# The fifth head pair of a top-k attention kernel without folded rows, and working rows in other buffers

## Chip, core and metric

One NeuronCore of a Trainium2 chip. The metric is the device time of one execution in microseconds. Its engines are PE (TensorE, matmuls; its weight loads are listed as PEld), DVE (VectorE), ACT (ScalarE), POOL (GpSimd) and SP, whose queue issues the DMAs. Each works through its own instructions in the order of the program and waits on semaphores for the others.

## What is computed

```
scores = q @ k.T / 8                              # B=8, H=8, S=576, D=64
kth    = 32nd largest score of each row
attn   = softmax of the scores >= kth, else 0     # per row of 576
x      = attn @ v, the heads side by side         # (8, 576, 512)
u      = x + (x.T @ U @ V).T                      # rank 32 mix over the sequence
out    = u + relu(u @ w1) @ w2                    # 512 -> 2048 -> 512
```

All in float32. The small weights U, V and w1, w2 come as float64 and are turned into float32 in the kernel, block by block (`next_params`, lines 216 to 231): three passes on ACT (L174, L175, L178), a shift on DVE (L186), two additions on POOL (L187, L189).

## The kernel before

Two heads of one batch entry make a pair, so there are 32 pairs, `g` = 0 to 31. A pair's 576 rows are cut into five row tiles, `t` = 0 to 4: four of 128 rows for both heads (two rows of 576 scores in each partition, `n` = 2), and a last one that holds the 64 leftover rows of both heads (one row in each partition). One step of the loop at lines 770 to 883 takes one row tile: step n is tile (n // 5, n % 5). Pair 4, the fifth, has steps 20 to 24; it is the first pair of the second batch entry. `ALONE` is 20: steps 0 to 19 run the first four pairs with no MLP behind them; steps 19 and 20 have a branch of their own (780 to 817); from then on the MLP of the batch entry that is done (`mlp`, 640 to 688) is dealt out as filler on PE by `fill` (742 to 760), a share to each call, by count and not by time. Its two matmul loops are L650 (u @ w1) and L669 (@ w2). So PE has filler from step 20 on.

A row tile passes through these stages, and a step issues stages of several tiles interleaved:

- `scores(g, t)` (312 to 358): PE multiplies (L322) into PSUM tiles `sc`; ACT copies to SBUF `Ssb`: L356 to L358 for pairs 0 to 4, L349 for the pairs from 5 on, which are `blocked` (line 285: g > 4; their q and k are laid out by a DVE transpose, L292, and their columns in another order), L339 for the last tile of any pair. Called one step ahead of `front`.
- `fold(g, t)` and `split(g, t)` (365 to 390): for folded pairs, each row of 576 is turned into 288 maxima `upper` and 288 minima `lower` of two halves: POOL adds the halves as integers (L387, in `fold`), DVE takes the maximum (L389, in `split`), POOL subtracts it from the sum (L390). L389 reads its first half from PSUM where `fronts_of` has it, which is set for blocked pairs and for each pair's last tile; else it reads both from SBUF. Both are called a step ahead of `front`, in the middle of the tile before; L389 thus lies in DVE's queue among that tile's passes.
- `front(g, t)` (409 to 499): the 32nd largest value of each row, in DVE instructions that find eight maxima (MAX8) or strike eight values out (MATCH_REPLACE8). Unfolded: MAX8 over 576 (L443), then three times a strike over 576 (L455) and a MAX8 (L460); the first strike writes to working rows `places`, so that the scores stay whole, and the later ones work in them. Folded: two MAX8 and a strike over `lower` (288; L429, L431, L433) put 16 candidates behind the 288 of `upper`, and then the same passes run over 304 values. A generator: each `next` issues one part. After the last MAX8, ACT scales the threshold (L482) and makes a gap for each row (L485), POOL takes it off (L488), ACT takes the exponential (L394). The first four pairs use other ways for some rows (`ways`, 396 to 404).
- `turns(g, t)` (529 to 550): PE transposes the weights (L543, L548), ACT copies them to `PT` (L544, L549). From step 31 on DVE and two DMAs do most of it (`blocks`).
- `values(g, t)` (558 to 590): PE multiplies with v (L577, L581; L567 for the last tile); ACT copies on (L590, L575). `inverse` (552 to 556) gives the reciprocals of the sums on DVE.
- `mixed(g, wait)` (593 to 638): the rank 32 mix of a pair (L602, L613, L625, L627 on PE; L606, L621, L635 on ACT).

Pools matter here. `hT` is a ring of 10 buffers of 128 x 640 floats that holds the MLP's hidden rows (line 660, written by ACT at L662) and, in pairs 0 to 3, the working rows (line 437). `upper` is a ring of 2 buffers of 128 x 2 x 304 floats, used by folded pairs alone. `lower` has one buffer.

Of the kernel before, what the change touches and what calls it, by code (L numbers as in the profile page):

```python
# [8 lines left out]
F32 = mybir.dt.float32  # L9
# [5 lines left out]
TOPK = 32  # L15
# [11 lines left out]
def kernel(  # L27
# [30 lines left out]
    P = 128  # L58
# [6 lines left out]
    HALF = S // 2  # L65
    assert S == MAIN + TAIL and D == 64 and H % 2 == 0 and C == 512 and TOPK % 8 == 0
    NPAIR = H // 2
    NP = B * NPAIR
# [8 lines left out]
    HT = 10  # L77
# [5 lines left out]
    attn = ctx.enter_context(tc.tile_pool(name="attn", bufs=2))  # L83
    small = ctx.enter_context(tc.tile_pool(name="small", bufs=8))
    mlpp = ctx.enter_context(tc.tile_pool(name="mlpp", bufs=2))
# [10 lines left out]
    WIDE = 2 * P + TAIL  # L96
# [184 lines left out]
    def blocked(g):  # L281

        return g > NPAIR
# [78 lines left out]

    def fold(g, t):

        if NPAIR <= g < NP:
            upper = attn.tile([P, 2, HALF + TOPK // 2], F32, tag="upper", name="upper")
            lower = attn.tile([P, 2, HALF], F32, tag="lower", name="lower", bufs=1)
            folds[g, t] = upper, lower  # L370
            pair(g, t, 0)
# [6 lines left out]
    def pair(g, t, stage):  # L378
        S2 = S2s[g, t]
        n = S2.shape[1]  # L380
        upper, lower = folds[g, t]
        top, bottom = upper[:, 0:n, 0:HALF], lower[:, 0:n].bitcast(U32)
        a, b = S2[:, :, 0:HALF], S2[:, :, HALF:S]
        if t < NT and blocked(g):
            a, b = (ends_of(probs[g, t], i) for i in range(2))
        if stage == 0:
            nc.gpsimd.tensor_tensor(bottom, a.bitcast(U32), b.bitcast(U32), ALU.add)  # L387
        else:
            nc.vector.tensor_tensor(top, fronts_of.pop((g, t), a), b, ALU.max)  # L389
            nc.gpsimd.tensor_tensor(bottom, bottom, top.bitcast(U32), ALU.subtract)  # L390

    def weigh(chunk, E, nmax, total=None):

        nc.scalar.activation(E, chunk, AF.Exp, bias=nmax, scale=SCALE, accum_out=total)  # L394

    def ways(g, t):

        if (g, t) == (NPAIR - 1, NT - 1):
            return (0,), (), (1,)
        if (g, t) == (NPAIR - 1, NT):  # L400
            return (0,), (), ()
        if t == NT:
            return (), (), (0,)
        return ((), (1,), (0,)) if g < NPAIR else ((), (), (1, 0))
# [4 lines left out]
    def front(g, t):  # L409

        if t == 0:
            dens[g] = small.tile([P, 2 * NT + 1], F32, tag="den", name="den", bufs=3)
        S2, den = S2s.pop((g, t)), dens[g]
        n = S2.shape[1]
        chunks = [S2[:, c] for c in range(n)]
        sums = [den[:, 2 * t + c : 2 * t + c + 1] for c in range(n)]
        first = small.tile([P, 2, 8], F32, tag="first", name="first", bufs=3)  # L420
        nmax = small.tile([P, 2], F32, tag="nmax", name="nmax", bufs=4)
        order = (1, 0) if n == 2 else (0,)
        folded = (g, t) in folds
        if folded:
            upper, lower = folds.pop((g, t))
            curs = [upper[:, c] for c in range(n)]
            spots = [[upper[:, c, HALF + i : HALF + i + 8] for c in range(n)] for i in (0, 8)]
            for c in order:
                nc.vector.max(spots[0][c], lower[:, c])  # L429
            for c in order:  # L430
                nc.vector.match_replace(lower[:, c], spots[0][c], lower[:, c], NEG)  # L431
            for c in order:
                nc.vector.max(spots[1][c], lower[:, c])  # L433
        else:
            curs = list(chunks)
            places = [
                mlpp.tile([P, 2, WIDE], F32, tag="hT", name="hT", bufs=HT)
                .rearrange("p c n -> p (c n)")[:, 0:S]
                for _ in range(n)
            ]  # L440
        ms = [first[:, c] for c in range(n)]
        for c in order:
            nc.vector.max(ms[c], curs[c])  # L443
        yield
        early, pooled, gaps = ways(g, t)
        for i in range(1, TOPK // 8):
            if i == 1:
                nc.scalar.mul(nmax[:, 0:n], first[:, 0:n, 0], -SCALE)
                Es = {c: attn.tile([P, S], F32, tag="E", name="E") for c in early}
                for c in early:  # L450
                    weigh(chunks[c], Es[c], nmax[:, c : c + 1])
            for c in order:

                nxt = places[c] if i == 1 and not folded else curs[c]
                nc.vector.match_replace(nxt, ms[c], curs[c], NEG)  # L455
                curs[c] = nxt
            m8 = small.tile([P, 2, 8], F32, tag="m8", name="m8", bufs=4)
            ms = [m8[:, c] for c in range(n)]
            for c in order:
                nc.vector.max(ms[c], curs[c])  # L460
            yield
        for c in pooled:
            gap = attn.tile([P, S], F32, tag="E", name="E")
            nc.gpsimd.tensor_scalar(gap, chunks[c], ms[c][:, 7:8], NEG, ALU.is_lt, ALU.mult)
            nc.gpsimd.tensor_tensor(chunks[c], chunks[c], gap, ALU.add)  # L465
        for c in early:
            nc.vector.scalar_tensor_tensor(
                out=chunks[c],
                in0=chunks[c],
                scalar=ms[c][:, 7:8],  # L470
                in1=Es[c],
                op0=ALU.is_ge,
                op1=ALU.mult,
                accum_out=sums[c],
            )
        if t == NT:
            del qkTs[g]
        yield
        if gaps:
            lo, hi = min(gaps), max(gaps) + 1  # L480
            least = small.tile([P, 2], F32, tag="least", name="least", bufs=3)
            nc.scalar.mul(least[:, lo:hi], m8[:, lo:hi, 7], WIDEN)  # L482
            for c in gaps:
                gap = attn.tile([P, S], F32, tag="E", name="E")
                nc.scalar.activation(  # L485
                    gap, chunks[c], AF.Relu, bias=least[:, c : c + 1], scale=-WIDEN
                )
                nc.gpsimd.tensor_tensor(chunks[c], chunks[c], gap, ALU.subtract)  # L488
            yield
        ahead = order[0:1] if len(gaps) == 2 else ()  # L490
        for c in ahead:
            weigh(chunks[c], chunks[c], nmax[:, c : c + 1], sums[c])
            yield
        for c in order:
            if c not in early and c not in ahead:
                weigh(chunks[c], chunks[c], nmax[:, c : c + 1], sums[c])
        if t == NT and g != NPAIR - 1:
            nc.scalar.activation(den, den, AF.Identity, bias=eps)
        yield
# [270 lines left out]
    for n in range(STEPS + 2):  # L770
        g, t = divmod(n, CH)
        if n < STEPS:
            if t == 0 and g + 1 < NP:
                load(g + 1)
            if t == 1 and g + 1 < NP:
                ready = prep(g + 1)
            fronts[n] = front(g, t)
            next(fronts[n])
        here, last = fronts.get(n, iter(())), fronts.pop(n - 1, iter(()))
        if n >= ALONE - 1 and n <= ALONE:  # L780

            if n < ALONE:
                next(last)
                values(*divmod(n - 3, CH))
                list(turning)
                next(here)
                next(last)
                scores(*divmod(n + 1, CH))
                fold(*divmod(n + 1, CH))
                values(*divmod(n - 2, CH))  # L790
# [11 lines left out]
            fill()  # L802
            scores(*divmod(n + 1, CH))
            fold(*divmod(n + 1, CH))
            next(here)
            while mixing:
# [12 lines left out]
        if n < ALONE:  # L819
            if ease:  # L820
                next(last, None)
            scores(*divmod(n + 1, CH))
            fold(*divmod(n + 1, CH))
            if n >= 3:
                values(*divmod(n - 3, CH))
                if (n - 3) % CH == NT:
                    mixing.append(mixed((n - 3) // CH, 3))
            list(turning)
            fill()
            next(here)  # L830
            if t < NT - 1:
                next_params(1)
            fill()
            next(ready, None)
            next(here)
            next(last, None)
            fill()
            split(*divmod(n + 1, CH))
            next(here)
            if t in (0, 1, NT - 1):  # L840
                next_params(1)
            next(here)
            fill()
            if n >= 1:
                turning = turns(*divmod(n - 1, CH))
            continue
# [70 lines left out]
```

## Time and profile before

| | |
|---|---|
| Median of 3 runs | 1743.06 us (1742.22 to 1745.01) |
| The profiled execution | 1742.03 us; its span 1740.2 us |
| Mean granted PE clock | 0.971 of full |
| L387 and L390 (POOL, fold) | 140 instructions each, means 1296 and 1287 ns |
| L389 in pair 4, both halves in SBUF | 0.76, 1.78, 1.80, 1.56 us |
| L443 over 576 values (unfolded) | 36 instructions, median 742 ns |
| L443 over 304 values (folded) | 252 instructions (126 rows of the list), median 459 ns |

The profile's second part cuts the span into 40 slices of 43.5 us and gives each engine's busy share in tenths. The waits name an instruction, what it waited for, and how long. The timelines list the instructions of one engine by start time. Two instructions in a row overlap a little in them, so that what one costs is best read from its start to the next one's start. Steps 20 to 24 take the stretch from about 203 to 256 us.

### The profile page before, as it was taken

The page shows a single profiled execution, that of the slowest core. Times are in us where ns is not written, and L with a number is a line of the kernel's source. Part 1 is how long each engine was busy: PE and PEld are TensorE (multiplying, and loading weights), DVE is VectorE, ACT ScalarE, POOL GpSimd, SP SyncE. Part 2 cuts the span into 40 slices and gives each one's busy share as a digit, 9 for nine tenths or more (in the row PEclk, how much of TensorE's full clock was granted, in tenths as well). Part 3 has the DMA queues.
Part 4 walks back from the last instruction along what each step waited for, and adds up shares of the span by engine and source line. Part 5 has one row for each costly group of instructions (what it writes and reads, how often), then busy time and mean ns, then how long its engine had stood idle before and what let it go on. Part 6 is the DMA issues. An engine that isn't in the chain of part 4 may idle for free.

```text
span 1740.2 us, 29711 instructions
## 1 busy us (share of the span) xinstructions
PE 1634.9 (94%) x9489; PEld 1208.1 (69%) x9489; DVE 1494.1 (86%) x4358; ACT 1023.9 (59%) x2582; POOL 956.7 (55%) x759
## 2 busy tenths in 40 slices
PE   4566789999999999999999999999999999999999
PEld 2344556777677876778677776687667876687677
DVE  7999889899999999999999999999999999993000
ACT  4888788665655666565656665565656656563100
POOL 4778688656555555555555555556555555552000
PEclk7788899999999999999999999999999999999999
DMA  3332222344434444444444444444444444432010
GB/s 87 91 90 83 73 73 64 78 111 119 119 99 116 117 114 107 112 116 105 118 101 117 114 111 105 112 111 115 110 107 119 114 109 103 117 90 70 4 16 13
DMA packets 275837, 167.37 MB, mean 96 GB/s; under 512 B 173920, under 2 KB 260192, under 8 KB 275680
## 3 DMA queue, kind: packets, MB, share of 16 engines
q1 hardware_dynamic: 274624, 165.20, 36.8%
q8 instruction: 75, 1.23, 0.3%
q14 instruction: 82, 0.67, 0.1%
q10 hardware_dynamic: 1056, 0.26, 0.1%
HBM read 101.42 MB, written 63.96 MB: 95 GB/s over the span
## 4 chain that ended last, share of the span: by engine, by line
PE 78%; DVE 11%; DMA 3%; ACT 3%; POOL 1%; issue 1%; SPq 1%; POOLq 0%; DVEq 0%; ACTq 0%
PE mm L669 27%; PE mm L650 26%; PE sc L322 8%; PE O L581 6%; DVE m L460 4%; DVE hT L455 4%; DMA PT<-away 2%; PE O L567 2%; PE up L625 2%; PE tp L548 1%; DVE first L443 1%; PE O L577 1%; PE tp L543 1%; DMA away<-y 1%; PE up L627 1%
## 5 line engine op out<-in xcount | busy, mean ns | idle before, releaser
L669 PE MATMUL mm<-hT,w 128*128 128x256 f32 (+1 forms) x2048 | 545.1, 411 | 0.0
L650 PE MATMUL mm<-uT,w 128*128 128x256 f32 (+1 forms) x2048 | 539.8, 411 | 0.0
L488 POOL TENSOR_TENSOR Ssb<-Ssb,E 128x576 f32<-128x576 f32 x271 | 378.7, 1415 | 283.5 <-ACT E L485 283.2
L650 PEld LDWEIGHTS mm<-uT,w 128*128 128x128 f32 x2048 | 376.0, 192 | 100.0 <-issue 13.3
L669 PEld LDWEIGHTS mm<-hT,w 128*128 128x128 f32 x2048 | 374.4, 192 | 94.7 <-issue 11.5
L460 DVE MAX8 m<-upper 128x8 f32<-128x304 f32 x756 | 323.7, 465 | 2.9
L390 POOL TENSOR_TENSOR lower<-lower,upper 128x576 uint32<-128x576 uint32 (+1 forms) x140 | 180.2, 1287 | 110.4 <-DVE upper L389 103.3
L394 ACT ACTIVATE Ssb<-Ssb,nmax 128x576 f32<-128x576 f32 x286 | 221.6, 779 | 17.4 <-POOL Ssb L465 9.6
L455 DVE MATCH_REPLACE8 upper<-m,upper 128x304 f32<-128x304 f32 x504 | 227.5, 458 | 0.0
L662 ACT ACTIVATE hT<-mm 128x320 f32<-128x320 f32 (+1 forms) x256 | 104.8, 409 | 203.5 <-PE mm L650 201.8
L387 POOL TENSOR_TENSOR lower<-Ssb 128x576 uint32<-128x576 uint32 (+1 forms) x140 | 181.5, 1296 | 69.5 <-ACT Ssb L349 23.5
L322 PE MATMUL sc<-qkT 64*128 64x288 f32 x1334 | 209.6, 437 | 8.6 <-ACT Ssb L356 7.8
L485 ACT ACTIVATE E<-Ssb,least 128x576 f32<-128x576 f32 x271 | 197.9, 769 | 5.2
L322 PEld LDWEIGHTS sc<-qkT 64*128 64x128 f32 x1334 | 115.4, 182 | 94.5 <-issue 42.6
L349 ACT COPY Ssb<-sc 128x576 f32<-128x576 f32 x216 | 127.1, 640 | 83.4 <-PE sc L322 82.1
L515 DVE STREAM_TRANSPOSE y<-Ssb 128x512 f32<-128x512 f32 x208 | 142.9, 702 | 22.8 <-ACT Ssb L394 20.9
L581 PE MATMUL O<-PT,va 128*64 128x128 f32 x2048 | 145.0, 285 | 8.5 <-DMA PT<-away 8.5
L429 DVE MAX8 upper<-lower 128x8 f32<-128x288 f32 x252 | 103.0, 445 | 38.3 <-POOL lower L390 38.3
L581 PEld LDWEIGHTS O<-PT,va 128*64 128x64 f32 x2048 | 113.5, 141 | 25.5 <-DMA PT<-away 10.8
L682 DVE TENSOR_TENSOR oT<-uT,mm 128x320 f32<-128x320 f32 (+1 forms) x8 | 3.6, 454 | 144.1 <-PE mm L669 144.1
L590 ACT COPY XT<-O 128x128 f32<-128x128 f32 x128 | 34.2, 267 | 143.3 <-PE O L581 143.2
L455 DVE MATCH_REPLACE8 upper<-first,upper 128x304 f32<-128x304 f32 x252 | 114.0, 459 | 0.0
(95 smaller groups left out, 2068.7 us busy)
## 6 DMA issues: line engine op xcount, KB each, us to landing
away<-y SPq DMA_DIRECT2D x416, 128.0 KB, 2.4
PT<-away SPq DMA_DIRECT2D x104, 512.0 KB, 3.3
raw<-in_moe_w_ch_dram SPq DMA_DIRECT2D x32, 512.0 KB, 3.9
va<-in_v_dram SPq DMA_DIRECT2D x64, 128.0 KB, 2.3
out_dram<-ob SPq DMA_DIRECT2D x57, 128.0 KB, 2.0
ld<-in_q_dram SPq DMA_DIRECT2D x108, 64.0 KB, 2.7
ld<-in_k_dram SPq DMA_DIRECT2D x108, 64.0 KB, 2.4
ld<-in_q_dram SPq DMA_DIRECT2D x108, 8.0 KB, 2.3
```

What stands on the lines that cost most here:

```text
L322: nc.tensor.matmul(out, lhsT=qkT[half(h), 0, cols(t)], rhs=qkT[half(h), 1, lo:hi], start=True, stop=True,)
L387: nc.gpsimd.tensor_tensor(bottom, a.bitcast(U32), b.bitcast(U32), ALU.add)
L390: nc.gpsimd.tensor_tensor(bottom, bottom, top.bitcast(U32), ALU.subtract)
L394: nc.scalar.activation(E, chunk, AF.Exp, bias=nmax, scale=SCALE, accum_out=total)
L455: nc.vector.match_replace(nxt, ms[c], curs[c], NEG)
L460: nc.vector.max(ms[c], curs[c])
L485: nc.scalar.activation(gap, chunks[c], AF.Relu, bias=least[:, c : c + 1], scale=-WIDEN)
L488: nc.gpsimd.tensor_tensor(chunks[c], chunks[c], gap, ALU.subtract)
L515: nc.vector.transpose(y[:, :, h].rearrange("p r c j -> p c r j"), E2[:, a : a + MAIN].rearrange("p (c r j) -> p c r j", c=NT, r=4),)
L581: nc.tensor.matmul(O[half(h)], lhsT=va[:, h, j, :], rhs=PB[:, h, j] if shared(g, t) else PT[:, NT * h + j], start=False, stop=(j == NT - 1),)
L650: nc.tensor.matmul(ph[:, 0:w], lhsT=w1[:, cc, f * P : (f + 1) * P], rhs=uT[:, cc, lo:hi], start=(cc == 0), stop=(cc == NC - 1),)
L669: nc.tensor.matmul(po[:, 0:w], lhsT=w2[:, f, c * P : (c + 1) * P], rhs=hTs[f][:, 0:w], start=(f == 0), stop=(f == NF - 1),)
```

## The change

Two lines. Pair 4 is no longer folded: `fold` takes the blocked pairs alone, which are those from 5 on, so `split` finds nothing for pair 4, and `front` goes its unfolded way there. The working rows of all unfolded pairs, now pairs 0 to 4, are taken from the ring `upper` of the pool `attn` and no longer from the ring `hT` of `mlpp`; of each buffer's 608 columns the first 576 are used. Nothing else in the program differs; the numbers of buffers are the same.

```diff
     def fold(g, t):
 
-        if NPAIR <= g < NP:
+        if blocked(g) and g < NP:
             upper = attn.tile([P, 2, HALF + TOPK // 2], F32, tag="upper", name="upper")
             lower = attn.tile([P, 2, HALF], F32, tag="lower", name="lower", bufs=1)
             folds[g, t] = upper, lower
@@
         else:
             curs = list(chunks)
             places = [
-                mlpp.tile([P, 2, WIDE], F32, tag="hT", name="hT", bufs=HT)
+                attn.tile([P, 2, HALF + TOPK // 2], F32, tag="upper", name="upper")
                 .rearrange("p c n -> p (c n)")[:, 0:S]
                 for _ in range(n)
             ]
```

## The prediction

> **What bounds the kernel now.** I read the busy shares first, then busy time in stretches of 5 us around the fifth pair (pair 4; its five row tiles are steps 20 to 24), then the waits there, then each engine's timeline.
>
> ```profile
> PE 1634.9 (94%) x9489; PEld 1208.1 (69%) x9489; DVE 1494.1 (86%) x4358; ACT 1023.9 (59%) x2582; POOL 956.7 (55%) x759
> PE   4566789999999999999999999999999999999999
> DVE  7999889899999999999999999999999999993000
> ```
>
> PE is the bound from about slice 6 on; before that DVE is full and PE is not. The fifth pair lies in the crossing (198 to 256 us). Time saved there reaches the end only as PE idle time removed: afterwards PE runs nearly without a gap (1480.9 of 1500 us from 240 on) in a fixed order.
>
> ```profile
> 195.00:200.00 5.00, 3.21 (x31) 2.13 (x27) 1.46 (x4) 3.89 (x10) 2.90 (x3) 1.00 0.34 53
> ...
> 220.00:225.00 5.00, 5.00 (x27) 3.27 (x26) 5.00 (x14) 3.63 (x8) 3.11 (x4) 1.00 0.00 0
> 225.00:230.00 5.00, 1.45 (x8) 0.78 (x6) 5.00 (x15) 3.71 (x8) 3.05 (x3) 1.00 0.36 105
> 230.00:235.00 5.00, 3.38 (x19) 2.46 (x21) 5.00 (x16) 3.66 (x11) 5.00 (x5) 0.65 0.36 107
> 235.00:240.00 5.00, 5.00 (x19) 3.35 (x16) 4.11 (x10) 2.34 (x7) 4.17 (x3) 0.67 0.15 45
> ```
>
> (PE, PEld, DVE, ACT, POOL busy us, then PE's granted clock.) PE loses 5.2 us in 225 to 235, and right after it runs at half clock.
>
> ```profile
> DVE upper L429 <- POOL lower L390: 14.0, 6, 4.7
> ...
> ACT least L482 <- DVE m L460: 4.9, 3, 2.6
> ...
> DVE upper L389 <- ACT Ssb L358: 3.5, 1, 3.5
> ```
>
> (195 to 330 us: who waited for whom, total us, times, longest.) The timelines of DVE, ACT and PE place them; a row is start, length, engine, line, operation, and in brackets the idle time ahead of it and what ended it. (4,0) is row tile 0 of pair 4.
>
> ```profile
> 198.60 0.76 DVE L389 TENSOR_TENSOR upper<-Ssb 128x576 f32<-128x576 f32 x1 [3.54 <-ACT Ssb L358]
> ...
> 216.09 0.82 DVE L429 MAX8 upper<-lower 128x8 f32<-128x288 f32 x2 [2.27 <-POOL lower L390]
> ...
> 239.28 0.82 DVE L429 MAX8 upper<-lower 128x8 f32<-128x288 f32 x2 [0.89 <-POOL lower L390]
> ...
> 226.25 0.20 ACT L482 ACTIVATE least<-m 128x2 f32<-128x2 f32 x1 [2.62 <-DVE m L460]
> ...
> 230.24 0.33 PE L548 MATMUL tp<-ident,Ssb 128*128 128x128 f32 x1 [3.79 <-ACT PT L544]
> ...
> 233.06 0.79 PE L577 MATMUL O<-PT,vd 128*128 128x128 f32 x2 [1.39 <-ACT PT L549]
> ```
>
> DVE stands before the fold of (4,0), in the middle of tile (3,4), and before (4,1) and (4,3). Being late, it keeps ACT waiting at L482 for the last MAX8 of (4,1). Queued behind L482 on ACT is the PT copy L544 (229.58) that PE's L548 needs; so PE stands 3.79 us, and 1.39 more for L549.
>
> [...] half clock from about 200.76 to 204.17 and from 231.48 to 238.31[...]. [...] the windows just ahead had PE busy 38% and 36%; one with 53% (224.6 to 228.1) left the clock alone.
> [...] L389 with both inputs in SBUF took 1.78, 1.80 and 1.56 us under POOL work, 0.76 free of it, and a mean 0.742 where one input is in PSUM.
>
> **The change, part by part** (profiled execution; DVE from start to start).
>
> 1. *DVE work.* An unfolded two-row tile, (3,3), runs from 181.88 to 191.52: 9.64 us. A folded one, (4,1), runs from 216.09 to 226.15, less 0.32 for L186 and 1.73 for the next tile's L389: 8.01. Single rows, waits and L186 taken out: 5.64 for (3,4) (0.78 for L443, then 1.68, 1.64, 1.54 for each L455 with its L460) against 5.15 for (4,4) (0.49, 0.55, 0.50, 0.51, then 1.02, 1.04, 1.04). The five L389 take 0.68 + 1.71 + 1.73 + 1.48 + 0.35 = 5.95. Removed: 4 x 8.01 + 5.15 + 5.95 = 43.1; added: 4 x 9.64 + 5.64 = 44.2. DVE gets 1.1 us more to do. Could the wide operations stretch beside POOL? The 36 wide L443 span 731 to 761 ns beside a POOL that was 78% busy (20 to 200 us), so no: at most 0.02 each, nothing below.
> 2. *DVE waits.* 3.54 + 2.27 + 0.89 = 6.7 us go. In their place L443 waits for ACT's copy (L358). It is there at 198.57 for (4,0), which DVE reaches at 199.2: no wait. Behind it are queued the two den operations for L575.
> 3. *POOL.* Five L387 and five L390 go: 1.97+1.41+1.41+1.59+0.79 and 1.41+1.40+1.42+1.39+0.80 = 13.6 us. POOL isn't the bound, but L488 stood behind them.
> 4. *Buffers.* Working rows move from hT to the two `upper` buffers. Writers and readers are all on DVE, in order; the waits are those of before. The MLP's first Relu into hT (213.22) didn't wait for DVE before either. Nothing. No DMA, no matmul and no ACT instruction is moved; SP's queue stays.
>
> **The path, step by step.**
> Step 19: DVE goes on at 195.05 without the stop and without L389, so L467 of (3,4) ends at 199.2 instead of 203.5. But PE was busy (at half clock) with L581 and L602 until 203.68 before that tile's transposes, so they don't move. Only L575, which waited for the reciprocal until 206.94, goes at 206.6: PE shifts by 0.3.
> Step 20: DVE does (4,0) in 9.64 + 0.25 (den) + 0.32 (L186) from 199.2 to 209.4. Copy (4,1) comes at 209.7: DVE waits 0.3.
> Step 21: (4,1) to 209.7 + 9.64 + 0.4 (L186) = 219.8 instead of 226.15. ACT, full from 218.9 on, comes to L482 at 223.2 and finds it ready. Its fixed chain (L482, L485 twice 1.59; L178 0.64; three copies 1.10; L544 0.48) ends at 227.0, so L548 starts at 227.2, not 230.24. L662 0.32, the second L544 0.53, L394 0.76 and L549 follow (POOL's L488, now behind L187 and L189 alone, is done at 225.5, and no longer holds L394): L577 starts at 229.05 instead of 233.06. That is 4.0 us.
> Clock: PE's idle in this stretch is then 1.1 + 0.55 us. No 3.41 us window is under 52% busy, just where the clock was kept before. Without half clock the run from L577 to the end of L650 x12 takes 4.76 us (0.32, 1.02 and 3.42 from the later rows) instead of 7.34: 2.6 us.
> Sum: 4.0 + 2.6 = 6.6 us.
> Steps 22 to 24: is DVE late now? (4,2) ends at 219.8 + 1.28 (L292) + 0.32 + 9.64 + 0.8 (L186) = 231.8; its L482 is due at 239.76 - 6.6 = 233.1. (4,3) takes 9.64 + 0.6 + 0.32 (two L186) to 242.4; its L482 is due at 250.28 - 6.6 = 243.7. For (4,4) the margin is 2.7. Cover of 1.3 us: if DVE takes more, that comes off the gain. From step 25 on rows are folded as before and everything (ACT, POOL, DVE) hangs on PE's order, so the shift stays.
> 1742.03 (span 1740.2 and 1.8 around it) - 6.6 = 1735.4; the median of the runs is 1.03 above the profiled execution: 1736.5.
>
> **Rivals.**
> B, *the clock still drops*: 52% is between 53% (kept) and 38% (dropped), and half a microsecond of further delay on ACT decides it. Then only the wait goes: 4.0 us, 1739.1. For it: the margin is thin[...]. Against: the two idle pieces have 1.2 us of work between them.
> C, *the gain is given back*: PE still stands 2.3 us in 280 to 300 (1.54 of it at 281.8, for L544) and 4.5 in 340 to 440. [...] half clock for one or two windows costs 1.7 to 3.4, and other waits realign: some 5 us back, 1741.5. Against: those waits hang on PE's own results.
> D, *slower, DVE becomes the bound*: place, steps 20 to 24. If the removed waits for POOL come back as waits for ACT's copies, DVE has only its longer tiles: 9.64 against 8.01 + 0.68 for an L389[...], 0.95 a tile, and 0.14 for the last: 4 us later at L482 and so at PE: 1747. It decides when ACT's copies come over 6 us later against DVE than computed. Against: copy (4,2) is there at 217.3 and DVE wants it at 221.4.
> That the change does nothing is excluded: the program has 10 POOL instructions and 20 rows of DVE's listing fewer.
>
> **Chances.** Forecast 0.55, B 0.23, C 0.15, D 0.07. Forecast's own range is 1733 to 1738.5: the unknown costs are 1.3 us of cover and the clock's 2.6; the runs span 1742.2 to 1745.0, and 0.2% (3.5 us) is about what can be told from no change. The range reaches over B and part of C: 1732.5 to 1742. Faster by over 0.2% (under 1739.6): 0.55 + over half of B = 0.68; within: the rest of B and C = 0.25; slower 0.07.
>
> **What would show it.** Right: no L387 or L390 before step 24; no DVE wait of 3.5 at 195; no ACT wait at L482 near 223; L577 of (4,0) near 229; PE's clock full after 204; DVE busy in 199 to 242. Wrong: PE idle over 2 us in 225 to 230, half clock at 231, or a DVE wait for L358 of over 1 us; then (B, D) the gain shrinks. If L577 is 4 us early but the end isn't, C holds.

## The result, and the profile after

| | before | changed |
|---|---|---|
| Median, first measurement | 1744.03 us (1742.22 to 1745.91, 4 runs) | 1737.41 us (1735.06 to 1737.89, 4 runs) |
| Ratio, 95% interval | | 0.9959 [0.9942, 0.9977] |
| Median, second measurement | 1742.93 us (1741.40 to 1744.65, 9 runs) | 1736.68 us (1733.63 to 1737.09, 5 runs) |
| Ratio, 95% interval | | 0.9961 [0.9947, 0.9974] |
| Profiled execution (span) | 1742.03 us (1740.2) | 1737.48 us (1735.6) |

The changed kernel is 6 to 7 us faster: 1737.4 where 1736.5 was forecast. The two profiled executions differ by 4.6 us only. One profile is one execution: two of the changed kernel have spans of 1735.6 and 1734.3, so the sum is judged by the medians and the steps by the places in the trace.

The page of the changed kernel, first its busy time, then the shares of the slices:

```profile
PE 1631.6 (94%) x9489; PEld 1205.1 (69%) x9489; DVE 1496.6 (86%) x4317; ACT 1024.0 (59%) x2582; POOL 942.7 (54%) x749
PE   4566899999999999999999999999999999999999
DVE  7999989999999999999999999999999999993000
```

DVE works 2.5 us longer and POOL 14.0 less. In the two slices from 174 to 261 us PE goes from 7 and 8 to 8 and 9, DVE from 8 and 8 to 9 and 8. The 5 us stretches of the changed kernel (PE, PEld, DVE, ACT, POOL busy us, then PE's clock):

```profile
195.00:200.00 5.00, 3.93 (x35) 2.65 (x35) 4.83 (x13) 4.61 (x13) 1.52 (x2) 1.00 0.32 52
220.00:225.00 5.00, 4.70 (x26) 2.83 (x24) 5.00 (x10) 4.97 (x11) 2.40 (x2) 1.00 0.32 105
225.00:230.00 5.00, 3.73 (x26) 2.57 (x27) 5.00 (x12) 4.36 (x14) 4.92 (x5) 1.00 0.32 105
230.00:235.00 5.00, 5.00 (x27) 3.13 (x26) 5.00 (x11) 4.45 (x10) 2.22 (x3) 1.00 0.33 107
235.00:240.00 5.00, 5.00 (x35) 3.71 (x34) 5.00 (x12) 4.35 (x13) 3.90 (x3) 1.00 0.01 3
275.00:280.00 5.00, 2.66 (x14) 1.46 (x15) 5.00 (x16) 3.78 (x9) 4.92 (x5) 0.76 0.32 105
```

In 225 to 235 PE now stands 1.27 us where it stood 5.2, at full clock. In the last row, 40 us later, PE stands 2.3 us and the clock drops; the profile of before has a shorter stop there and full clock. In the waits of 195 to 330 the row of L389 for L358 is gone, and the ones left are of later, folded tiles but for one of 0.43 us:

```profile
DVE upper L429 <- POOL lower L390: 10.6, 4, 4.7
...
ACT least L482 <- DVE m L460: 4.0, 3, 2.3
```

The timelines of PE and ACT (start, length, line, and in brackets the idle time ahead and what ended it; the row of 283.34 is of the kernel before, the others of the changed one):

```profile
206.22 1.24 PE L322 MATMUL sc<-qkT 64*128 64x288 f32 x8
...
225.73 0.33 PE L548 MATMUL tp<-ident,Ssb 128*128 128x128 f32 x1 [1.03 <-ACT PT L544]
...
227.67 0.49 PE L577 MATMUL O<-PT,vd 128*128 128x128 f32 x2 [0.54 <-ACT PT L549]
...
232.54 1.19 PE L322 MATMUL sc<-qkT 64*64 64x288 f32 x8
...
277.20 0.71 PE L613 MATMUL pT<-x,U 128*32 128x128 f32 x10 [2.58 <-POOL w L189]
...
283.34 0.60 PE L613 MATMUL pT<-x,U 128*32 128x128 f32 x10 [1.54 <-ACT PT L544]
...
221.75 0.19 ACT L482 ACTIVATE least<-m 128x2 f32<-128x2 f32 x1
232.44 0.20 ACT L482 ACTIVATE least<-m 128x2 f32<-128x2 f32 x1 [0.43 <-DVE m L460]
```

L482 of (4,1) finds its MAX8 done, L548 waits 1.03 us instead of 3.79, and the scores of (4,4), the 64x64 row, start at 232.54 instead of 240.40. The releaser named at L613 in the changed kernel is not the true one. L613 reads x and U, which no L189 of this stretch writes, and it writes to a buffer of the ring that L544 empties. In every trace of the study this L613 starts 0.73 to 0.74 us after ACT's L544 does (here L544 at 276.47 and L613 at 277.20, before 282.60 and 283.34), while L189 only happened to end at 277.15.

What PE's lead over before is, at the same instruction in both profiles:

| instruction on PE | before | changed | lead |
|---|---|---|---|
| scores of (4,1), L322 | 207.96 | 206.22 | 1.7 |
| L577 of (4,0) | 233.06 | 227.67 | 5.4 |
| scores of (4,4), L322 | 240.40 | 232.54 | 7.9 |
| scores of (5,1), L322 | 259.44 | 252.24 | 7.2 |
| L613 of step 26 | 283.34 | 277.20 | 6.1 |
| scores of (5,4), the x10 row | 293.66 | 288.39 | 5.3 |
| span | 1740.2 | 1735.6 | 4.6 |

So between these two executions 7.9 us are won by 240, and 2.6 are given back by 290.

### The profile page after: what moved, and what is told of

It is laid out like the page before. It is cut to its first block, busy times and chain, and to the rows that moved or that the text cites. A ratio compares the mean times of both kernels' runs of the same rounds, so it can differ in the third digit from the quotient of the medians.

```text
span 1735.6 us, 29654 instructions
## 1 busy us (share of the span) xinstructions
PE 1631.6 (94%) x9489; PEld 1205.1 (69%) x9489; DVE 1496.6 (86%) x4317; ACT 1024.0 (59%) x2582; POOL 942.7 (54%) x749
## 4 chain that ended last, share of the span: by engine, by line
PE 78%; DVE 13%; DMA 4%; ACT 3%; issue 1%; POOL 1%; SPq 1%; POOLq 0%; DVEq 0%
PE mm L650 26%; PE mm L669 26%; PE sc L322 8%; PE O L581 6%; DVE upper L455 5%; DVE m L460 5%; DMA PT<-away 3%; PE O L567 2%; DVE first L443 2%; PE up L625 2%; PE tp L548 1%; PE O L577 1%; PE tp L543 1%; PE up L627 1%; DMA away<-y 1%
## 5 line engine op out<-in xcount | busy, mean ns | idle before, releaser
L488 POOL TENSOR_TENSOR Ssb<-Ssb,E 128x576 f32<-128x576 f32 x271 | 379.0, 1416 | 291.0 <-ACT E L485 290.6
L460 DVE MAX8 m<-upper 128x8 f32<-128x304 f32 (+1 forms) x864 | 407.8, 509 | 3.6
L455 DVE MATCH_REPLACE8 upper<-m,upper 128x304 f32<-128x304 f32 (+1 forms) x576 | 285.4, 502 | 0.0
L390 POOL TENSOR_TENSOR lower<-lower,upper 128x576 uint32<-128x576 uint32 (+1 forms) x135 | 173.8, 1287 | 108.8 <-DVE upper L389 101.6
L662 ACT ACTIVATE hT<-mm 128x320 f32<-128x320 f32 (+1 forms) x256 | 104.9, 410 | 201.6 <-PE mm L650 200.0
L322 PE MATMUL sc<-qkT 64*128 64x288 f32 x1334 | 209.3, 436 | 8.0 <-ACT Ssb L356 7.2
L387 POOL TENSOR_TENSOR lower<-Ssb 128x576 uint32<-128x576 uint32 (+1 forms) x135 | 174.2, 1290 | 63.1 <-ACT Ssb L349 23.2
L322 PEld LDWEIGHTS sc<-qkT 64*128 64x128 f32 x1334 | 115.1, 182 | 93.6 <-issue 42.7
L429 DVE MAX8 upper<-lower 128x8 f32<-128x288 f32 x243 | 99.2, 444 | 34.8 <-POOL lower L390 34.8
L455 DVE MATCH_REPLACE8 upper<-first,upper 128x304 f32<-128x304 f32 x243 | 109.8, 459 | 0.0
```

The source lines that it names most:

```text
L322: nc.tensor.matmul(out, lhsT=qkT[half(h), 0, cols(t)], rhs=qkT[half(h), 1, lo:hi], start=True, stop=True,)
```

## The experiments

The theories by the letters of the expectations. **W**, the prediction's: DVE's stops at folded tiles make L482 late, so PE stands at L548 and loses its clock. **P**: what counts is POOL's 14 us less. **B**: the other buffers. **H**: the longest stop, 3.5 us ahead of (4,0), is the head of the queue and worth most. **L**: what counts is L389 with both inputs in SBUF, which three times took 1.56 to 1.80 us in pair 4. **S**: DVE has slack after the change. **A**: the gap at L613 eats part of the gain. Ratios are against the kernel before, with 95% intervals; what a run saves is worked out from its ratio, and 0.001 of it is 1.7 us.

**The buffers alone.** Pair 4 folded as before, the working rows of pairs 0 to 3 in `upper`.

```diff
-                mlpp.tile([P, 2, WIDE], F32, tag="hT", name="hT", bufs=HT)
+                attn.tile([P, 2, HALF + TOPK // 2], F32, tag="upper", name="upper")
```

> Only the second half of the change: the working rows of pairs 0 to 3 lie in the two upper buffers, pair 4 is still folded. Theory W (the stops of DVE at the folded tiles delay ACT's L482, PE's gap and its half clock follow): nothing, 0 +- 1.5 us against before; the gap of 3.8 us at L548 and the half clock at 231 stay. Rival B (the buffers do it, by freeing hT for the MLP): about -6 us.

Measured: 1742.51 us, ratio 0.9996 [0.9986, 1.0005]. B falls: the second of the two edits alone does nothing that can be told. Its PE timeline:

```profile
203.59 0.63 PE L543 MATMUL tp<-ident,Ssb 128*128 128x128 f32 x4 [1.18 <-DVE Ssb L467]
...
230.78 0.48 PE L548 MATMUL tp<-ident,Ssb 128*128 128x128 f32 x1 [3.79 <-ACT PT L544]
```

The 3.79 us at L548 are those of before. The first row matters more: here PE waits 1.18 us for DVE in step 19, which the profile of before does not show. Two more places differ from the profile of before, though the kernels are equally fast:

```profile
283.11 0.60 PE L613 MATMUL pT<-x,U 128*32 128x128 f32 x10 [2.07 <-POOL w L189]
...
296.22 1.20 PE L322 MATMUL sc<-qkT 64*64 64x288 f32 x10
```

L613 waits 2.07 us and not 1.54, half clock follows from 283.9 to 290.8, and the scores of (5,4) start at 296.22 and not at 293.66. So this place changes by more than 2 us between two profiles of kernels that are equally fast.

**POOL kept busy.** The changed kernel, with additions and subtractions on POOL into an idle buffer at the places of L387 and L390.

```diff
+        elif g == NPAIR:
+            idle[g, t] = attn.tile([P, 2, HALF], F32, tag="lower", name="lower", bufs=1)
+            load_pool(g, t, 0)
...
+        elif (g, t) in idle:
+            load_pool(g, t, 1)
```

> The changed kernel, with POOL's ten instructions put back as idle work: at the old places of L387 and L390 of pair 4, POOL adds the halves and subtracts one of them again, 13 us in all, and nothing reads the result. It leaves out no part of the computation. Theory W: DVE's order is that of the changed kernel, so most of the gain stays, -4 to -6.5 us against before; up to 2 lost where POOL's weight additions and L488 come later. Rival P (the gain is POOL's relief): back to before, -1 to +1.

Measured: 1737.68 us, 0.9967 [0.9954, 0.9980]: the changed kernel's time, and the scores of (4,4) at 232.67 against 232.54. P falls.

**Only tile (4,0) unfolded.**

```diff
-        if NPAIR <= g < NP:
+        if NPAIR <= g < NP and (g, t) != (NPAIR, 0):
```

> Only row tile 0 of pair 4 unfolded, tiles 1 to 4 folded; working rows in hT as before. It takes away the longest stop of DVE (3.54 us at 195, before L389 of (4,0)). Theory W: the second stop takes its place, since L390 of (4,1) waits on POOL behind the additions L187 and L189 and is not sooner than about 215.5: (4,1) still starts near 216, L482 still waits some 2.6 us, 0 to -1.5 us against before. Rival H (the longest stop, an L389 at the head of DVE's queue in the middle of tile (3,4), is the cause): -3 to -4.5.

Measured: 1739.92 us, 0.9983 [0.9975, 0.9990], 3.0 us less. Its timelines of DVE, ACT and PE:

```profile
214.94 0.82 DVE L429 MAX8 upper<-lower 128x8 f32<-128x288 f32 x2 [2.52 <-POOL lower L390]
...
225.11 0.20 ACT L482 ACTIVATE least<-m 128x2 f32<-128x2 f32 x1 [2.64 <-DVE m L460]
...
229.10 0.47 PE L548 MATMUL tp<-ident,Ssb 128*128 128x128 f32 x1 [3.81 <-ACT PT L544]
```

The wait is W's: with the first stop gone, the second (2.52 us ahead of (4,1)) holds L482 as long as before, 2.64 us, and PE stands 3.81 us. The size is not: W had 0 to 1.5 us for this, H 3 to 4.5, and the interval is 1.7 to 4.4. In the trace the whole row of events lies 1.1 us earlier, since the scores of (4,1) start at 206.80 and not at 207.96, so the stop's own effect in step 19 was taken too small. By the scores of (4,4) the lead is 2.5 us (237.90 against 240.40), because the half clock, 227.5 to 234.3, falls in part into the gap ahead of L548.

**Only tiles (4,1) to (4,4) unfolded.** `if (blocked(g) or (g, t) == (NPAIR, 0)) and g < NP:` in `fold`, the buffers as in the change.

```diff
-        if blocked(g) and g < NP:
+        if (blocked(g) or (g, t) == (NPAIR, 0)) and g < NP:
```

> The other part: row tiles 1 to 4 of pair 4 unfolded, tile 0 folded; working rows in upper. The stop of 3.54 us at 195 stays. Theory W: (4,0) ends near 212, (4,1) follows at once and ends near 222, which is before ACT comes to L482: PE's gap at L548 falls to about 1 us, the half clock at 231 goes; then DVE is the tighter one in steps 22 and 23: -3.5 to -6 us against before. Rival H: the longest stop is still there, -1 to -3.

Measured: 1735.98 us (6 runs), 0.9959 [0.9943, 0.9975], 7.1 us less, with an interval of 4.4 to 9.9: as far as the runs can tell as much as the whole change. Its DVE, ACT and PE timelines:

```profile
198.93 0.76 DVE L389 TENSOR_TENSOR upper<-Ssb 128x576 f32<-128x576 f32 x1 [3.87 <-ACT Ssb L358]
...
223.83 0.19 ACT L482 ACTIVATE least<-m 128x2 f32<-128x2 f32 x1
...
227.82 0.33 PE L548 MATMUL tp<-ident,Ssb 128*128 128x128 f32 x1 [1.06 <-ACT PT L544]
```

H, which had 1 to 3 us for this, falls as the main cause: the longest stop is there in full, 3.87 us, and L482 waits for nothing. What has to go above all is the stop at (4,1), in the tile that L482 waits for. The stop at (4,0) still costs: the scores of (4,4) start at 234.60, against 232.54 in the changed kernel. At that place the leads over before roughly add up, 2.5 us for (4,0) alone, 5.8 for the rest alone, 7.9 for both; the medians (3.0, 7.1, and 6.2 to 7.1) are too wide to say otherwise.

**Folded, but L389 with one input from PSUM.** This kernel and the next read the first half of pair 4's rows from PSUM, where the second head's row begins with other columns. They change that part of the computation: for that head DVE's maxima are taken over other pairs of scores than POOL's sums, so what they compute for it is not what the kernel before computes. The instructions are as many, and only L389 changes its length.

```diff
+        if g == NPAIR:
+            fronts_of[g, t] = scs[0][:, :, 0:HALF]
         main = S2.rearrange("p (h n) -> p h n", h=2)
```

> The kernel before, all of pair 4 folded, but its L389 reads the first half from PSUM, as it does in later pairs, so POOL doesn't stretch it. Theory W: L389 falls from 1.7 to 0.74 us in three tiles, but the stops at 195, before (4,1) and before (4,3) stay: (4,1) ends some 1.6 us sooner, PE's gap at L548 shrinks from 3.8 to about 2: -1 to -2.5 us against before, -4 if the clock is kept. Rival L (the stretched L389 are what costs, DVE's sum of work decides): 3 us less DVE work show one to one and the gain is as large as that of the change, -5 to -7.

Measured: 1740.52 us, 0.9987 [0.9979, 0.9994], 2.3 us less. L389 shrinks to 0.73 to 0.76 us from 1.56 to 1.80. In the profile of before the three long ones (210.38, 222.76, 235.18) started beside a POOL instruction and ended 0.61 to 0.62 us after it; the one of (4,0) started 0.04 us ahead of POOL's L387 (198.60 against 198.64), so not free of POOL as the prediction has it, and took 0.76; one of pair 5, with half its input in PSUM, took 0.76 beside POOL's L488 (253.73). But the stop grows to fill much of what is won:

```profile
216.04 0.82 DVE L431 MAX8 upper<-lower 128x8 f32<-128x288 f32 x2 [3.13 <-POOL lower L392]
...
225.14 0.20 ACT L484 ACTIVATE least<-m 128x2 f32<-128x2 f32 x1 [1.03 <-DVE m L462]
```

(Lines are 2 higher here.) DVE gets to (4,1) as late as POOL's subtraction lets it; within (4,1) the shorter L389 brings L482 1.1 us forward (225.14 against 226.25). L falls as the main cause: 2.3 of 7 us, with an interval of 1.0 to 3.7.

**Tile (4,0) unfolded and the rest with L389 from PSUM.**

```diff
+        if g == NPAIR and t > 0:
+            fronts_of[g, t] = scs[0][:, :, 0:HALF]
...
+        if NPAIR <= g < NP and (g, t) != (NPAIR, 0):
```

> A mix: tile 0 of pair 4 unfolded (working rows in hT), tiles 1 to 4 folded with L389 reading from PSUM. DVE has about 3 us less to do than in the changed kernel, but the stops before (4,1) and (4,3), which wait on POOL's L390, are back. Theory W: stops count for more than work: -1 to -3.5 us against before, less than the change brings. Rival L (DVE's sum of work decides): better than the change, -7 to -9.

Measured: 1739.59 us, 0.9982 [0.9976, 0.9989], 3.1 us less. The stop ahead of (4,1) is 1.95 us long, the one ahead of (4,3) 1.34, L482 waits 0.98, and PE 2.17 at L548. Without the stretched L389 and without the first stop, about half of the gain is there (1.9 to 4.2 of 6.2 to 7.1 us), though DVE has less to do than in the changed kernel. So, by these waits, what the rest hangs on is mostly the fold's way over POOL and back.

**The clock alone.** The kernel before with matmuls that do no work of the result, in the gap ahead of L548 of (4,0). The first form wrote to a new PSUM tile:

```diff
+        if n == ALONE + 2:
+            warm = ps_m.tile([P, C], F32, tag="mm", name="mm")
+            for i in range(6):
+                nc.tensor.matmul(
+                    warm[:, 0:WIDE], lhsT=w1[:, 0, 0:P], rhs=V[:, 0:WIDE], start=(i == 0), stop=(i == 5)
+                )
```

> The kernel before with six matmuls (12 records of 0.27 us, 3.3 us in all) that nobody reads, put on PE into the gap ahead of L548 of step 22. It leaves out no part of the computation. It fills the gap with activity and takes no wait away. If half clock after the gap costs what the prediction took (2.6 us from L577 to the end of the twelve L650): half clock at 231 gone, -1.5 to -3 us against before. If the clock costs nothing, 0 to +0.5; if the six don't fit into the gap, up to +1.

Measured: 1743.73 us, 1.0006 [0.9998, 1.0013]. It tells nothing on the clock, since the gap is not filled:

```profile
231.16 5.19 PE L863 MATMUL mm<-V,w 128*128 128x320 f32 x12 [4.12 <-ACT hT L662]
```

The new tile waits for a buffer that ACT's L662 frees, and on ACT L662 stands behind L482 as well. The second form writes to columns of the tile that the MLP has open at that time, which nothing reads:

```diff
+        if n == ALONE + 2:
+            warm = opened[0][:, WIDE:C]
+            for i in range(8):
+                nc.tensor.matmul(
+                    warm, lhsT=w1[:, 0, 0:P], rhs=V[:, 0 : C - WIDE], start=False, stop=False
+                )
```

> The kernel before with eight matmuls that nobody reads (16 records of about 0.16 us, 2.6 us) in the gap ahead of L548 of step 22. Unlike the first try they write to the unused columns of the PSUM tile that is open there, so they wait for nothing on ACT. It leaves out no part of the computation, and takes no wait away. If the half clock after the gap costs what the prediction took (2.6 us from L577 to the end of the twelve L650): no half clock near 231, -1.5 to -3 us against before[...]. If the clock costs nothing: 0 +- 0.7.

Measured: 1742.27 us against 1742.03, 1.0003 [0.9995, 1.0011]. Its PE and ACT timelines:

```profile
226.84 2.76 PE L866 MATMUL mm<-V,w 128*128 128x192 f32 x16
...
283.12 0.60 PE L613 MATMUL pT<-x,U 128*32 128x128 f32 x10 [2.54 <-POOL w L189]
...
239.02 0.20 ACT L482 ACTIVATE least<-m 128x2 f32<-128x2 f32 x1 [1.04 <-DVE m L460]
```

The clock is at 1.00 from 220 to 245. From L577 (233.64) to the scores of (4,4) (238.51) it takes 4.87 us instead of 7.34, just what the changed kernel takes (227.67 to 232.54). In the runs nothing of these 2.5 us is left (0.9 us less to 1.9 more). The trace shows where they go in one execution. PE is 1.9 us ahead at the scores of (4,4), the next L482 waits 1.04 us, and 1.2 us of lead are left at 277. Then L613 stands 2.54 us, half clock follows from 284.0 to 290.8, and the scores of (5,4) start at 296.27, 2.6 us later than in the profile of before. So the kept clock alone is worth nothing at the end. That it would be worth 2.5 us if DVE were early too was not tested by itself.

**More work for DVE.** The changed kernel with one more MAX8 over 576 for each of the nine rows of pair 4, 9 x 0.66 = 5.9 us.

```diff
+        if g == NPAIR:
+            more = small.tile([P, 2, 8], F32, tag="more", name="more", bufs=2)
+            for c in order:
+                nc.vector.max(more[:, c], chunks[c])
         for c in order:
             nc.vector.max(ms[c], curs[c])
```

> The changed kernel with a MAX8 over 576 more for each row of pair 4 on DVE, nine in all, 0.66 us each (6 us), whose result nobody reads. It leaves out no part of the computation. Theory W with DVE just covered (the changed trace shows L482 waiting 0.43 us in step 22 and not elsewhere in steps 21 to 23, and POOL's L187 behind DVE's L186): the 6 us come through less about 1: +3.5 to +5.5 us against the changed kernel. Rival S (DVE has slack in these steps, PE or ACT sets the time): at most +1.5.

Measured: 1739.64 us, 0.9984 [0.9977, 0.9991]: 2.8 us less than before, so about 4 us of the gain are lost for 5.9 us of work. (L482 is L486 here.) ACT:

```profile
223.04 0.20 ACT L486 ACTIVATE least<-m 128x2 f32<-128x2 f32 x1 [0.34 <-DVE m L464]
235.99 0.20 ACT L486 ACTIVATE least<-m 128x2 f32<-128x2 f32 x1 [1.79 <-DVE m L464]
247.29 0.20 ACT L486 ACTIVATE least<-m 128x2 f32<-128x2 f32 x1 [2.09 <-DVE m L464]
```

S falls: the work comes back as waits at L482, and half clock follows from 252.3 to 259.1. The cover of steps 22 to 24 is then some 2 us, and DVE is the tight engine there after the change.

**The changed kernel once more**, for the interval and a second profile.

> The changed kernel once more, unaltered, for a narrower interval and a second profile[...]. Theory W: -5.5 to -7.5 us against before (ratio 0.9957 to 0.9969). The stop of 2.6 us before L613 near 274 is in the order of the program and is there again[...].

Measured: as in the first table. The longer gap at L613 is there again:

```profile
276.69 0.60 PE L613 MATMUL pT<-x,U 128*32 128x128 f32 x10 [2.49 <-POOL w L189]
...
279.14 1.43 PE L625 MATMUL up<-V,Tb 128*128 128x320 f32 x2 [1.01 <-ACT Tb L621]
```

Half clock follows from 279.1 to 282.5. The changed kernel with POOL kept busy waits only 1.53 us there, so this gap is not the same in all kernels with the change.

**One weight block a step later.** Ahead of the L544 that L613 waits for, ACT passes two blocks of weights in step 26 (L178 at 271.28, L174, L175, and L178 at 274.77). In the changed kernel the second is moved out of that step, in pair 5 alone:

```diff
-        if t in (1, 3):
+        if t in ((2, 3) if g == NPAIR + 1 else (1, 3)):
             next_params(1)
```

> The changed kernel, but pair 5 takes its second extra weight block in its third step instead of its second, so that step 26 has one block's three passes on ACT instead of two. The changed trace gives back 2.6 us between 274 and 288: PE stands 2.58 us before L613, for a PT copy that is queued behind those passes on ACT, and then runs at half clock. Theory A (ACT's queue in step 26 causes the give-back): the gap falls to 1 us or less, no half clock there: -2 to -3.5 us against the changed kernel, -8.5 to -10.5 against before. Rival (DVE's and POOL's chain of pair 4 and 5 sets it): 0 to -1 against the changed kernel; or, if w2 then comes too late for L669, slower by 1 to 2.

Measured: 1732.54 us (1730.62 to 1734.14, 5 runs) against 1742.03, 0.9947 [0.9933, 0.9960]: 9.2 us less. PE:

```profile
275.90 0.60 PE L613 MATMUL pT<-x,U 128*32 128x128 f32 x10 [1.56 <-ACT PT L544]
```

The gap is 1.56 us, as in the profile of before and not under 1 as expected, and the clock stays full to 300. Against the changed kernel PE is 0.3 us ahead at the scores of (4,1), 1.3 at L613 and 3.1 at the x10 scores (285.33 against 288.39): 1.0 us from the wait and 1.8 from the clock. So what is queued on ACT sets that gap, as A says, and the gap costs the changed kernel time. The size is less sure: the medians are 4 to 5 us apart, but the two weren't measured side by side, one run of the changed kernel (1733.63) lies below this kernel's slowest, and the ratios' intervals overlap. That the gap eats part of what the change won is not shown. The kernel with the other buffers alone has a gap of 2.07 us and half clock there too, and the block was not moved in the kernel before, where it may win as much.

**The same, with (4,0) folded.**

```diff
-        if blocked(g) and g < NP:
+        if (blocked(g) or (g, t) == (NPAIR, 0)) and g < NP:
...
-        if t in (1, 3):
+        if t in ((2, 3) if g == NPAIR + 1 else (1, 3)):
```

> Row tile 0 of pair 4 folded, tiles 1 to 4 unfolded, and the weight block of pair 5 moved by a step as in the run beside it. Theory A: -9 to -11 us against before, as good as or a little better than with all five unfolded. Rival: as the run without the move, about -7.

Measured: 1734.21 us (1731.91 to 1736.28, 5 runs), 0.9955 [0.9942, 0.9967]: 7.8 us less, under the 9 to 11 expected. L613 waits 1.55 us and the clock is full. The interval, 5.7 to 10.1 us, reaches into what was expected. In the trace the scores of (4,1) start 2.1 us later than in the kernel above (208.02 against 205.92) and those of (5,4) 1.8 later (287.10 against 285.33): the stop at (4,0) costs here too. The kernel above has the lowest median of the study, 1.7 us lower, but the runs of the two overlap.

## Why the prediction was right, point by point

- *DVE's work, 1.1 us more*: 2.5. The wide passes kept their length, as argued (0.66 to 0.73 us from start to start). What was off is L186: 1.04 and 1.03 us in tiles (4,0) and (4,1), where 0.3 to 0.4 was taken, 1.4 us in all. Both times POOL was at work as it started (the last section has the rows). Tile (4,1) ended at 220.73, not at 219.8. (The mean of L389 with one input in PSUM is 0.744 us and not 0.742; nothing hangs on it.)
- *DVE's stops, 6.7 us, go, and no new wait for L358*: right. DVE waits for nothing from 190 to 250.
- *POOL and buffers, nothing*: right within some 2 us, by the two runs on P and B.
- *Step 19, 0.3 us*: **the term that failed**; it was 1.7. The prediction let the transposes of (3,4) wait for PE's own work until 203.68, at half clock. That half clock (200.8 to 204.2) was of the one profiled execution. In the profiles of six other kernels that fold (4,0) the clock is full there (in four of them it is halved just after, from 205 to 209), and L543 waits 1.18 to 1.19 us for DVE's L467. So the stop does hold PE where the clock is full, and the profile of before hid it. The 0.3 us by way of L575 came (0.37); the other 1.4 are the transposes, which start at 202.31 and not at 203.68.
- *Step 21, L577 4.0 us earlier*: 5.4. Without step 19 that is 4.0 - 0.3 = 3.7 predicted and 5.4 - 1.7 = 3.7 measured.
- *The clock, 2.6 us*: 2.5 (7.34 against 4.87) between the two profiles; against the profile of the other buffers alone, where the half clock falls in part into the gap, 1.2 (6.05 against 4.87). Rival B, that it drops all the same, did not come. But as a term that adds to the others it was put too simply: by itself it is worth nothing that the runs show.
- *Steps 22 to 24, a cover of 1.3 us*: just enough. L482 of (4,2) waits 0.43 us, the others not, and PE's lead is 7.9 us at the scores of (4,4) and of (5,0) alike.
- *"From step 25 on ... the shift stays"*: **between these two profiles this failed.** Of 7.9 us, 2.6 are given back: 0.7 by 252, 1.1 at L613, and the rest behind it, where the clock is halved. PE is 7.9 us earlier, but POOL's L390 of (5,0), behind the weight blocks in its queue, only 5.9 (252.67 against 258.57), and DVE and ACT with it: L482 of (5,0) waits 2.25 us instead of 0.96. Not all hangs on PE's order. This is rival C in its place, and with its half clock, at half its price of 5 us. But the profile of before happens to keep the clock at this place. Against that of the other buffers alone, a kernel as slow as before, the lead is 7.1 us at the scores of (4,4) (239.65) and 7.8 at those of (5,4) (296.22): nothing is given back. How much the change itself gives back stays open.

The two misses, 1.3 us too little up to 240 and 2.6 too much after it, partly cancel in the profiles: 7.9 - 2.6 = 5.3 against 6.6. The medians, which don't hang on one execution, give 6.2 to 7.1 (1742.93 - 1736.68; 0.41% of 1744). So the main mechanism was right (runs on (4,0), (4,1) to (4,4), P, B and DVE's load). That the sum came closer than its terms is in part luck, of errors that cancel and of the two executions that were profiled. Rival D is excluded: with 5.9 us more work for DVE the kernel was still 2.8 us faster than before. But DVE becomes the tight engine after only some 2 us of it. What of the last 0.7 us between the scores of (5,4) and the end belongs to the change is open: two profiles of the changed kernel differ by more.

## What to carry over

When the engine ahead of the bound does a round trip over another engine, look for the tile that the next wait hangs on: with the stops of (4,1) to (4,4) gone most of the gain was there (5.8 of 7.9 us at the scores of (4,4)), with the longest stop gone alone 2.5. Time saved early on the bound engine can be lost again at a later wait, as were the 2.5 us of the kept clock; look for the next wait that becomes the last one, and move work that isn't urgent out of that queue. A profile is one execution: a clock drop in it can hide a wait that others have (1.18 us at L543), and a drop that it lacks can make a later loss look like one of the change. Compare several profiles of before, too.

## What the runs showed of the hardware

- Half clock came after steps in which PE was busy 24 to 53% of the time. The stretch from 190 to 330 us of the fourteen profiles was cut into steps of 3.41 us, the length of the shortest half clock (200.76 to 204.17 in the profile of before), in line with the drops. At full clock, all eleven steps with PE busy 24 to 40% were followed by half clock (39%, where the prediction has 38, and 36% ahead of 200.76 and 231.48 in the profile of before, 24% ahead of 277.56 in the one of the changed kernel), and none with 54% and more. Between 42 and 53% both came: 12 steps lost the clock and 6 kept it. Examples are 52% lost (197.7 us, more work for DVE) and 42% kept (225.6 us, the first of the two kernels with added matmuls). The share of busy time alone doesn't decide there. Once at half clock, steps with 53 to 86% stayed there, and those from 89% on went back to full. The prediction judged the clock by such windows of 3.41 us; that it is decided in them was not shown.
- Nor does the length of a gap alone decide. Ahead of L613 in step 26, gaps of 1.50 to 1.56 us left the clock full in four kernels, and 1.51 to 1.53 us halved it in three; all of 2 us and more there halved it. Ahead of L548 and L577, gaps of 2.22 and 1.41 us (L389 from PSUM) left the clock alone, gaps of 2.17 and 1.42 (the same with (4,0) unfolded) halved it. What else decides was not shown.
- Striking and finding over 576 values beside POOL at work kept their 0.73 to 0.76 us, while L389 with two inputs in SBUF took up to 1.80. L186, a shift of 512 values, took between 0.38 and 1.20 us from 190 to 330 in the two profiles of before and changed, and the long ones started beside POOL at work:

```profile
203.61 1.04 DVE L186 TENSOR_SCALAR w<-w 128x512 uint32<-128x512 uint32 x1
...
203.32 1.04 POOL L607 TENSOR_TENSOR x<-x,den 128x512 f32<-128x512 f32 x1 [6.80 <-ACT x L606]
```

This L186 ends 0.28 us after POOL's L607, and so do those of 214.22 and 244.95 after a POOL instruction that ran as they started. In the fourteen profiles, none of the 213 that started with POOL standing took over 0.42 us; of the 148 that took over 0.45, 133 ended 0.28 to 0.29 us after such a POOL instruction (29, 21 and 19 in the two profiles of before and changed). In those two, 20 more of 512 values started beside a POOL instruction and took 0.40 to 0.43 us; why is open.
